# Windowed attention with sinks and a gated MLP on one core: the order of all five queues, the engines of movable work and the PSUM banks written out as tables in place of a list scheduler

## The chip, the cores and the metric

The kernel runs on one core of one Trainium2 chip. Its time is the device time of one execution in microseconds (us); less is better. A core has five engines, each with an instruction queue of its own that is worked through in order: TensorE (PE, matmuls; its weight loads are shown as PEld), VectorE (DVE), ScalarE (ACT), GpSimd (POOL) and SyncE (SP, which here only issues DMAs). They tell each other of finished work through semaphores. PSUM, where matmuls leave their results, has 8 banks of 128 partitions x 2 KB; in this kernel POOL reads none of them.

## The reference, cut to what matters

Attention over 4 batches x 8 heads x 768 positions with head size 64, in which a query sees the first 4 positions (sinks) and the 128 newest; then a gated MLP over the 3072 tokens with d_model 512 and d_ff 2048.

```python
B, H, S, D = q.shape                                   # 4, 8, 768, 64
scores = (1.0 / np.sqrt(D)) * np.matmul(q, k.transpose(0, 1, 3, 2))
rel = pos[:, None] - pos[None, :]
keep = (pos[None, :] < 4) | ((rel >= 0) & (rel < 128))
a = softmax(np.where(keep, scores, -1e9))              # over the last axis
x = np.matmul(a, v).transpose(0, 2, 1, 3).reshape(3072, 512)
h = x @ w_in                                           # 512 -> 2048
g = h * (1.0 / (1.0 + np.exp(-beta * h)))
out = g @ w_out                                        # 2048 -> 512
```

## The kernel before

**The work.** The tokens are cut into 8 half batches (hb, and T_ in the MLP) of 384 tokens. Attention goes by units: unit u is a pair of heads in half batch u // 4, so hb 0 has units 0 to 3, and so on to 31. The groups of matmuls on PE have these names here:

- T (lines 773 to 800, units 0 to 11): six transposes on PE that make q and k of a unit head-size-major, and their copy out of PSUM. From hb 3 on a DMA transpose does this (XP, line 764, called X).
- S (SC, 869 to 971): a burst of score matmuls for one to three tiles (L930, and L885 for the narrow bands from unit 8 on). Each tile takes two PSUM banks; ACT takes the exponential of both (E, L947), and DVE or POOL multiplies or selects the mask (L956, L966 on DVE, L962 on POOL; from unit 8 on most masks can be done on POOL alone). SS (L978, L982) is the same for the sink keys of a half batch.
- A (AV, 1005 to 1044): attention times v for one unit, or for four units as a quad (L1007, L1023, L1034), then a reciprocal and a multiplication on DVE (L1038, L1040).
- R (OT, 1046 to 1065): the result transposed into xT, on PE with a copy by DVE or ACT for units 0 to 11, later by a DMA transpose that SP issues (L1054).
- H (HQ, 1070 to 1088): four matmuls of 384 columns (L1078) for one block m of 16 of one tile T_; ACT's tanh (L1084) and DVE's product g (L1086) follow. H2.15 is T_ 2, m 15. There are three buffers for t and three for g.
- O (OQ, 1093 to 1121): g times w_out for tile 0 and the last third of tile 7, four matmuls at a time (L1102). O0.1.2 is tile 0, third 1, quarter 2.
- W (WP, 1228 to 1279): all other thirds go in pairs, a pair by seven products of half the size (L1245, eight matmuls of 256 columns each) instead of eight. W3.6 is product 6 of pair 3. The products need sums and differences of g (s_op, L1167) on DVE or POOL and of w_out (w_sums, L1150), and additions behind them (L1253). Pairs 0, 1, 3, 4, 6, 7, 9 are inside tiles 1 to 7; pairs 2, 5 and 8 join the last thirds of tiles 1 and 2, 3 and 4, 5 and 6.

**Loads and casts.** SP issues the loads of q, k and v (line 656), of the weights in 16 pieces (load_w, L668) and the DMA transposes; ACT issues the four loads of k of hb 0. The casts to bf16 (cast, cast_w, lines 571 to 577) run on ACT, DVE or POOL.

**What sets the order.** _program (431) calls these functions in an order that is partly written out ("early", "later", lines 1509 to 1525) and partly decided by background() (1387), which lets loads, casts and sums in when a running estimate says so. take() and choose() (528 to 562) give PSUM banks by the same estimate. Each call records operations with an estimated duration and, for movable work, a choice of engines (any_of, 500). Then Graph.arrange() (176 to 292) builds all queues anew: a list scheduler that keeps an estimated clock for each engine and for DMA, may take one of the next 3 to 10 groups of PE, picks for movable work the engine that would be done first, keeps POOL and some DVE operations (lock) apart, and puts in fill matmuls (L1494) in the first 18 us. resolve() (294) turns dependences into semaphore waits; a wait for work on the same engine is dropped for PE, and for the others unless it reads what was written.

The order that came of it on PE, from T5 on:

```
T5 T4 T7 H0.0 H0.1 T6 H0.2 H0.3 S[5,6] SS H0.4-0.6 S[7,8] H0.9 H0.7 H0.8 H0.10 S[9,10] H0.11-0.14 A5 A4 A6 A7 H0.15
O0.0.0 O0.1.0 R4 O0.2.0 O0.0.1 R5 R6 O0.1.1 R7 O0.2.1 H1.0-1.9 O0.0.2 T8 T9 O0.1.2 O0.2.2 T10 S[11,12] O0.0.3 T11
O0.1.3 O0.2.3 S[13,14] S[15] SS H1.10-1.12 A8 A9 H1.13 R8 H1.14 A10 A11 H1.15 R9 W0.1 R10 W0.2 W0.6 R11 W0.7 H2.0
S[16,17,18] SS W0.5 W0.4 W0.3 H2.1 S[19,20,21] H2.2-2.8 A12-15 H2.9-2.15 W1.1 S[22,23,24] W1.6 W1.2 W1.7 S[25,26] SS
W1.5 W1.4 A16 A17 H3.0 H3.1 W1.3 A18 A19 W2.1 H3.2 H3.3 W2.6 W2.2 H3.4-3.6 W2.7 H3.7 W2.5 H3.8 H3.9 W2.4 H3.10-3.12
W2.3 H3.13-3.15 W3.1 S[27,28,29] SS W3.2 W3.6 W3.5 W3.7 S[30,31,32] W3.4 H4.1 H4.2 H4.0 H4.3-4.7 W3.3 H4.8-4.15 A20-23
W4.1 W4.6 W4.2 S[33,34,35] W4.7 W4.5 W4.4 S[36,37] SS W4.3 W5.1 H5.0 H5.1 A24 H5.2 W5.6 H5.3 A25 A26 A27 W5.2 W5.7
H5.4 W5.5 H5.5-5.14 W5.4 H5.15 W5.3 W6.1 S[38,39,40] SS W6.2 W6.6 H6.0 S[41,42,43] W6.7 H6.1-6.7 A28-31 W6.5 W6.4
H6.8-6.15 W6.3 H7.0 W7.1 H7.1 H7.2 W7.6 W7.2 W7.7 W7.5 H7.3-7.5 W7.4 W7.3 H7.6 W8.1 H7.7 H7.8 W8.6 H7.9 W8.2 H7.10
H7.11 W8.7 H7.12-7.15 W8.5 W8.4 W9.1 W8.3 W9.6 W9.2 W9.7 W9.5 W9.4 W9.3, then the last third of tile 7 (O7.2, twice four)
```

Of the kernel before, what the change touches and what calls it, by code (L numbers as in the profile page):

```python
# [22 lines left out]
class Op:  # L23
    __slots__ = ("eng", "fn", "deps", "signal", "count", "waits", "sem", "vc", "dma", "seq", "end", "ns", "alts",
                 "group", "tail", "hold", "lock", "chain", "preds", "ready", "left", "succ", "at")


class Graph:

    ENGINES = ("pe", "act", "dve", "gp", "sp")
    HOP = 180
    SKIP = 3
    PAD = 100
    STRICT = 1
    WIDE, EARLY = 10, 60000
    SLACK = 0  # L40
    YIELD = 500
    COLD, WARM = 217, 150

    def __init__(self):
        self.ops = []
        self.writers = {}
        self.readers = {}
        self.last_x = {}
        self.free = {e: 800.0 for e in self.ENGINES}
        self.dma_free = 2500.0  # L50
        self.stalls = [(16000.0, 1100.0), (34000.0, 700.0)]
        self.port = {"gp": 0.0, "dve": 0.0}
        self.gaps = {"act": [], "dve": [], "gp": []}
        self.group = 0
        self.filler, self.fill_to = None, 0

    def begin(self):

        self.group += 1

    def add(self, eng, fn, ns=0, r=(), w=(), x=(), dma=None, alts=None, after=(), hold=550, chain=None, lock=False):

        o = Op()
        if alts:
            fn, ns = alts[eng]
        o.eng, o.fn, o.dma, o.ns, o.alts = eng, fn, dma, ns, alts or {eng: (fn, ns)}
        o.signal, o.count, o.waits, o.vc, o.hold, o.chain = False, 0, [], None, hold, chain
        o.group = self.group if eng == "pe" else None  # L70
        o.lock = lock
        o.seq = len(self.ops)
        deps = []
        for k in r:
            ws = self.writers.get(k)
            assert ws, k
            deps += [(p, True) for p in ws]
        for k in w:
            deps += [(p, False) for p in self.readers.get(k, ())]
            deps += [(p, False) for p in self.writers.get(k, ())]  # L80
        for k in after:
            deps += [(p, False) for p in self.readers.get(k, []) + self.writers.get(k, [])]
        for k in x:
            deps += [(p, False) for p in self.last_x.get(k, ())]
        o.deps = deps
# [5 lines left out]
        for k in x:  # L91
            self.last_x[k] = [o] if eng == "pe" else self.last_x[k] + [o]
        o.at = 0.0
        self.place_early(o, eng)
        self.ops.append(o)
        return o

    def ready_at(self, o, eng):
        return max([0.0] + [p.end + (0 if p.eng == eng and not p.dma else self.HOP) for p, _ in o.deps])

    def slot(self, eng, t, ns):

        for i, (a, b) in enumerate(self.gaps[eng]):
            if max(a, t) + ns <= b:
                return max(a, t), i
        return max(self.free[eng], t), None

    def place_early(self, o, eng):

        if eng in ("pe", "sp") or o.dma:  # L110
            self.place(o, max(self.free[eng], self.ready_at(o, eng)))
            return
        if o.alts and len(o.alts) > 1:
            best = None
            for e, (fn, ns) in o.alts.items():
                at, i = self.slot(e, self.ready_at(o, e), ns)
                if best is None or at + ns < best[0]:
                    best = (at + ns, e, at, i)
            _, eng, at, i = best
            o.eng = eng  # L120
            o.fn, o.ns = o.alts[eng]
        else:
            at, i = self.slot(eng, self.ready_at(o, eng), o.ns)
        gaps = self.gaps[eng]
        if i is None:
            if at > self.free[eng] + 50:
                gaps.append((self.free[eng], at))
                del gaps[:-40]
            self.free[eng] = at + o.ns
        else:  # L130
            a, b = gaps.pop(i)
            gaps[i:i] = [g for g in ((a, at), (at + o.ns, b)) if g[1] - g[0] > 50]
        o.at, o.end = at, at + o.ns

    def fill(self, fn, r):

        def one():
            o = Op()
            wide = self.free["pe"] + 2 * self.filler[0] <= self.fill_by
            o.eng, o.fn, o.dma, o.ns = "pe", fn[wide], None, self.filler[0] * (1 + wide)  # L140
            o.signal, o.count, o.waits, o.vc, o.lock = False, 0, [], None, False
            o.deps = [(p, True) for k in r for p in self.writers[k]]
            return o
# [19 lines left out]
    def at(self, keys):  # L163

        t = 0.0
        for k in keys:
            ws = self.writers.get(k)
            if not ws:
                return None
# [1405 lines left out]
```

## Time and profile before

| what | value |
|---|---|
| three runs | 222.39 us median, 221.91 to 224.91 |
| the profiled execution's own time | 221.55 us |
| its span in the profile | 219.8 us |
| granted TensorE clock | 1.00 |
| DMA moved | 39.92 MB, mean 182 GB/s |

The span runs from the first to the last instruction that the profile shows. Its page gives busy time by engine, then groups of instructions by line; further views give busy time by stretch, the chain of waits that ended last (a piece is start, length, what), and the timeline, where brackets say how long the engine was idle before a piece and what ended that. A matmul's busy time includes its way through the array, so matmuls in a row overlap and busy times add up to less than the sum of their lengths. DVE, ACT and POOL instructions in a row overlap a little, too.

### The profile page before, as it was taken

The numbers are of one execution on the slowest core, as the hardware profiler recorded it, in microseconds if no ns is written. First come the engines' busy times: TensorE is split into PE (matmuls) and PEld (weight loads), VectorE is DVE, ScalarE is ACT, GpSimd is POOL, SyncE is SP. The second block draws the span as 40 slices with busy tenths as digits, with TensorE's granted clock in tenths as the row PEclk, the third lists the DMA queues.
The fourth block names the chain that finished last, engine by engine and source line by source line (L and its number), as shares of the span: only waits on it lengthen the run. The fifth ranks groups of instructions, "written<-read, shape, count | busy, mean of one in ns | idle before, by whom it ended". The sixth has DMA issues, their size and how long they took to land.

```text
span 219.8 us, 5396 instructions
## 1 busy us (share of the span) xinstructions
PE 209.0 (95%) x2155; PEld 141.5 (64%) x2155; DVE 173.8 (79%) x375; ACT 152.8 (70%) x261; POOL 82.7 (38%) x136
## 2 busy tenths in 40 slices
PE   8899999998988999899998999999999999999995
PEld 3456547554456756578765766778676576777883
DVE  2686999899697549999868598999885698957850
ACT  3698996896993998767567797585959837355401
POOL 7225560382651693080011691582006930010010
DMA  6999999999969999899649999669947233120023
GB/s 186 251 329 369 352 277 372 364 282 220 194 156 179 217 148 260 139 184 215 144 123 228 221 109 220 125 134 244 145 102 171 44 86 84 48 94 6 0 99 143
DMA packets 94721, 39.92 MB, mean 182 GB/s; under 512 B 82072, under 2 KB 89512, under 8 KB 94696
## 3 DMA queue, kind: packets, MB, share of 16 engines
q1 hardware_dynamic: 91928, 33.28, 70.4%
q0 software_dynamic: 1680, 5.51, 7.4%
q10 hardware_dynamic: 1088, 0.79, 1.1%
q8 instruction: 17, 0.28, 0.6%
q14 instruction: 8, 0.07, 0.1%
HBM read 27.37 MB, written 6.29 MB: 153 GB/s over the span
## 4 chain that ended last, share of the span: by engine, by line
PE 54%; DVE 20%; DMA 10%; SPq 7%; ACT 6%; issue 2%
PE P L1245 22%; PE P L1078 22%; DVE g L1086 9%; SPq L656 5%; DMA g<-in_moe_w_in_dram 4%; DMA g<-in_moe_w_out_dram 4%; PE P L1102 4%; PE P L1034 3%; ACT t L1084 3%; ACT E L947 2%; DMA v_stage<-in_v_dram 2%; PE P L885 2%; DVE g L1167 1%; DVE onorm L1040 1%; SPq L668 1%
## 5 line engine op out<-in xcount | busy, mean ns | idle before, releaser
L1078 PE MATMUL P<-xT,w_in 128*128 128x384 bf16 x512 | 91.3, 326 | 2.0 <-DVE g L1086 0.8
L1084 ACT ACTIVATE t<-P,hbeta 128x384 f32<-128x384 f32 x128 | 70.9, 590 | 28.3 <-PE P L1078 19.3
L1086 DVE SCALAR_TENSOR_TENSOR g<-t,P 128x384 bf16<-128x384 f32 x128 | 67.2, 548 | 20.0 <-ACT t L1084 16.8
L1078 PEld LDWEIGHTS P<-xT,w_in 128*128 128x128 bf16 x512 | 48.4, 98 | 33.9 <-DVE g L1086 3.4
L962 POOL TENSOR_SCALAR_AFFINE_SELECT E<-E 128x512 bf16<-128x512 bf16 x57 | 39.2, 715 | 28.8 <-ACT E L947 28.6
L947 ACT ACTIVATE E<-P 128x1024 bf16<-128x1024 f32 x44 | 43.3, 1033 | 3.7 <-PE P L885 3.4
L1245 PE MATMUL P<-w_out,g 128*128 128x256 bf16 x240 | 30.7, 273 | 1.4 <-DVE g L1086 1.1
L1276 POOL DMA_DIRECT2D out_dram<-osb x18 | 9.9, 549 | 58.6 <-DVE osb L1253 58.5
L1245 PEld LDWEIGHTS P<-w_out,g 128*128 128x128 bf16 x240 | 22.7, 98 | 6.1 <-DVE g L1086 1.8
L1040 DVE TENSOR_TENSOR onorm<-P,rden 128x384 bf16<-128x384 f32 x32 | 17.6, 555 | 0.7
L1102 PE MATMUL P<-w_out,g 128*128 128x512 bf16 (+2 forms) x80 | 15.3, 337 | 0.0
L1253 DVE TENSOR_TENSOR osb<-P,wst 128x256 f32<-128x256 f32 x30 | 12.2, 417 | 3.7 <-PE P L1245 3.5
L1034 PE MATMUL P<-vaug,E 128*128 128x65 bf16 x352 | 14.4, 193 | 0.0
L1034 PEld LDWEIGHTS P<-vaug,E 128*128 128x128 bf16 x352 | 13.6, 97 | 1.1
L1494 PE MATMUL P<-const-bfloat16-1.0 128*128 128x512 bf16 (+1 forms) x37 | 10.9, 417 | 0.8 <-PEq L1557 0.8
L1245 PE MATMUL P<-v_stage,g 128*128 128x256 bf16 x80 | 10.4, 273 | 0.4 <-DVE wst L1253 0.4
L1253 DVE TENSOR_TENSOR wst<-P,wst 128x256 f32<-128x256 f32 x20 | 8.3, 417 | 2.8 <-PE P L1245 2.8
L1245 PE MATMUL P<-wst,g 128*128 128x256 bf16 x80 | 10.4, 273 | 0.0
L1102 PEld LDWEIGHTS P<-w_out,g 128*128 128x128 bf16 x80 | 6.9, 98 | 5.2
L571 ACT ACTIVATE k<-k_stage 128x512 bf16<-128x512 f32 (+1 forms) x12 | 7.4, 616 | 3.7 <-DMA k_stage<-in_k_dram 3.7
L956 DVE TENSOR_TENSOR E<-E,maskS 128x512 bf16<-128x512 bf16 x16 | 7.6, 487 | 2.0 <-ACT E L947 2.0
L571 ACT ACTIVATE wst<-P 128x256 f32<-128x256 f32 x9 | 3.4, 383 | 8.1 <-PE P L1245 8.0
(99 smaller groups left out, 259.4 us busy)
## 6 DMA issues: line engine op xcount, KB each, us to landing
v_stage<-in_v_dram SPq DMA_DIRECT2D x24, 256.0 KB, 5.3
out_dram<-osb POOLq DMA_DIRECT2D x21, 256.0 KB, 3.4
q_stage<-in_q_dram SPq DMA_DIRECT2D x15, 256.0 KB, 5.2
k_stage<-in_k_dram SPq DMA_DIRECT2D x15, 256.0 KB, 5.2
wst<-in_moe_w_in_dram SPq DMA_DIRECT2D x5, 512.0 KB, 8.1
wst<-in_moe_w_out_dram SPq DMA_DIRECT2D x4, 512.0 KB, 7.9
g<-in_moe_w_out_dram SPq DMA_DIRECT2D x4, 512.0 KB, 6.6
q_stage<-in_q_dram SPq DMA_DIRECT2D x2, 768.0 KB, 7.7
```

Source lines behind the costliest of these rows:

```text
L656: add("act" if hb == 0 and n == "k" and Q2 else "sp", lambda e: e.dma_start(dst, src), ns, w=keys, dma=f"d{n}{z}{'' if i is None else i}", ...
L947: add("act", lambda e, src=src, dst_=dst_: e.activation(dst_, src, AF.Exp, bias=0.0, scale=SCALE), act_ns(1024), w=[("E", z)] + [("m", z, ...
L962: alts = {"gp": (lambda e, dd=dd, sg=sg: e.affine_select(dd, dd, [[0, n] for n in dd.shape[1:-1]] + [[sg, 128]], ALU.is_ge, 0.0, base=min( ...
L1034: e.matmul(A[:, c0:c0 + D + 1], E[t_ % NE][:, i, hh, :], vaug[vz][:, kb % NK, 2 * hp + hh, :], start=a, stop=o, skip_group_check=True), 31,
L1040: add("dve", lambda e: e.tensor_tensor(onorm[on][:, :, :, :].rearrange("p m h d -> p (m h) d"), av[:, :, 0:D], rden[on][:, :].unsqueeze(2) ...
L1078: add("pe", lambda e, c=c: e.matmul(hp, w_in16[:, c, m * 128:(m + 1) * 128], xT[:, c, t0:t0 + HALF], start=(c == 0), stop=(c == 3)), mm_ns ...
L1084: add("act", lambda e: e.activation(tt[ti][:, :], hp, AF.Tanh, bias=0.0, scale=hbeta[:, m:m + 1]), act_ns(HALF) + 93, r=["hbeta"], w=[("t" ...
L1086: add("dve", lambda e: e.scalar_tensor_tensor(gt[T_ % NG][:, m, :], tt[ti][:, :], 1.0, hp, ALU.add, ALU.mult), dve_ns(HALF), r=[("t", ti)] ...
L1102: add("pe", lambda e, m=m: e.matmul(P[:, bk, 0:n], gt[T_ % NG][:, m, t * 128:(t + 1) * 128], w_out16[:, m, cols], start=(m == 0), stop=(m ...
L1245: add("pe", lambda e, i=i: e.matmul(P[:, bk, 0:HN], lhs[:, i, :], rhs[:, i, :], start=p in (1, 6, 5, 4) and i == 0, stop=i == 7, skip_grou ...
L1253: add("dve", lambda e: e.tensor_tensor(d, src, u, ALU.add), 310, r=r, w=w, x=[("B", bk)], after=after)
L1494: G.fill([lambda e, n=n: e.matmul(P[:, 7, 0:128 * n], one.to_broadcast([128, 128]), one.to_broadcast([128, 128 * n]), start=True, stop=Tru ...
```

## The change

The list scheduler, the estimates, the choice of banks and background() are gone. In their place stand four tables: SCRIPT, one letter a call, says in which order the functions record their operations; PE_ORDER says the order of the groups on PE, one letter a group, with the fill matmuls (f, F) in it; BANKS gives the PSUM bank of each take; QUEUES lists for ACT, DVE, POOL (gp) and SP the recorded operations in order, two base-36 digits each, and thereby their engine. What the functions compute, and their tiles, are as before. In resolve() a wait for work on the same engine is now dropped for PE alone.

```diff
-    G = Graph()
-    _program(nc, G, sb, ps, q, k, v, moe_w_in, moe_w_out, moe_beta, out)
-    G.arrange()
+    G = Graph(BANKS)
+    fillers = _program(nc, G, sb, ps, q, k, v, moe_w_in, moe_w_out, moe_beta, out)
+    G.order(PE_ORDER, QUEUES, fillers)
     G.resolve()
...
+class Bank(int):
+    def __new__(cls, bank):
+        b = super().__new__(cls, bank)
+        b.last, b.used = [], False
+        return b
...
+    def take(self, n):
+        return [Bank(next(self.banks)) for _ in range(n)]
...
+    def order(self, pe, queues, fillers):
+        last, at = {}, {}
+        lists = {e: [] for e in self.ENGINES}
+        for c in pe:
+            if c in fillers:
+                lists["pe"].append(self.new("pe", fillers[c]))
+                continue
+            i = at[c] = at.get(c, -1) + 1
+            while not self.by_kind[c][i]:
+                i = at[c] = i + 1
+            for o, takes in self.by_kind[c][i]:
+                for t in takes:
+                    if not t.used and t in last:
+                        o.deps += [(p, False) for p in last[t].last]
+                    t.used = True
+                    last[int(t)] = t
+                lists["pe"].append(o)
+        for e, s in queues.items():
+            for i in range(0, len(s), 2):
+                o = self.loose[int(s[i:i + 2], 36)]
+                o.eng, o.fn = e, o.alts[e]
+                lists[e].append(o)
...
     def resolve(self):
...
-                if not p.dma and p.eng == o.eng and (p.eng == "pe" or not raw):
+                if not p.dma and p.eng == o.eng == "pe":
                     continue
...
+PE_ORDER = ("FFFFFFFFFFF.FFF.FFF..FFFF..Ff....FF.FFFf...FFf..f.FF.Ff.BTTTTHHSHHSHHHHSHHHHHHHHAAARAOORRROHHHHOHHHO"
...
+QUEUES = {"act": ("010z03050718131b151e171k1l1n1q1w1z1t3334352a372d2e2f2k3g3u3n3d3h3y413l3j3x4f3p4c3v44464p4m484a3a4k4i"
...
-    for c in later:
...
+    for c in SCRIPT:
+        do(c)
+    return fillers
```

Read out with the groups' names, PE's order from T4 on is now:

```
T4 T5 T6 T7 H0.0 H0.1 S[5,6] SS H0.2 H0.3 S[7,8] H0.4-0.7 S[9,10] H0.8-0.15 A4 A5 A6 R4 A7 O0.0.0 O0.1.0 R5 R6 R7 O0.2.0
H1.0-1.3 O0.0.1 H1.4-1.6 O0.1.1 O0.2.1 H1.7 O0.0.2 O0.1.2 O0.2.2 T8 T9 T10 O0.0.3 O0.1.3 H1.8 T11 H1.9-1.15 O0.2.3
S[11,12] W0.1 S[13,14] W0.6 W0.2 W0.7 S[15] SS W0.5 W0.4 A8 A9 W0.3 A10 R8 A11 R9 R10 S[16,17,18] SS R11 H2.0-2.15
S[19,20,21] W1.1 W1.6 W1.2 W1.7 W1.5 W1.4 A12-15 W1.3 W2.1 W2.6 W2.2 S[22,23,24] W2.7 W2.5 W2.4 S[25,26] SS W2.3 A16 A17
H3.0-3.4 A18 H3.5 A19 H3.6-3.15 H4.0-4.8 W3.1 S[27,28,29] SS W3.6 W3.2 W3.7 S[30,31,32] W3.5 H4.9-4.14 W3.4 H4.15 W3.3
W4.1 A20-23 W4.6 W4.2 W4.7 S[33,34,35] W4.5 W4.4 W4.3 S[36,37] SS W5.1 W5.6 W5.2 H5.0-5.7 W5.7 H5.8-5.10 A24 H5.11-5.14
W5.5 A25 H5.15 A26 A27 W5.4 W5.3 W6.1 S[38,39,40] SS W6.6 W6.2 W6.7 S[41,42,43] W6.5 H6.0-6.15 W6.4 A28-31 W6.3 W7.1 W7.6
W7.2 W7.7 W7.5 W7.4 W7.3 W8.1 W8.6 H7.0-7.15 W8.2 W8.7 W8.5 W8.4 W8.3 W9.1 W9.6 W9.2 W9.7 W9.5 W9.4 W9.3, then O7.2
```

Instructions by kind of work and engine, where they differ (DMA issues are on the same engines as before):

| work | ACT | DVE | POOL |
|---|---|---|---|
| casts of q, k, v | 33 to 26 | 32 to 23 | 9 to 25 |
| casts of weights | 5 to 6 | 6 to 6 | 6 to 5 |
| masks | - | 31 to 24 | 57 to 64 |
| sums of g (L1167) | - | 38 to 34 | 2 to 6 |
| sums of w_out (L1150) | - | 5 to 6 | 3 to 2 |
| copies to xT (R) | 11 to 8 | 1 to 4 | - |
| copies and additions of O and W | 20 to 19 | 55 to 56 | - |

On the queues that matter beside PE: ACT casts weight pieces 8 and 9 behind H0.12, 10 behind H0.15, 13 behind H1.3 and 15 behind H1.4; before, 9 behind H0.14, 12 behind R4, 13 behind R6 and 14 behind R7. POOL has, behind its first weight sum, two q casts of hb 2 and then its second weight sum, where it had a weight sum, one q cast and a weight sum; and it does all six casts of q and k of hb 3 before the masks of S[11,12] to S[15]. SP issues the third v load of hb 2 and the sink values of batch 2 behind the first DMA transpose of hb 3, and mixes v loads and transposes differently later; its order up to the last weight load is unchanged. In a run of H groups ACT's and DVE's tables follow the groups, with neighbours exchanged here and there (H2.1 before H2.0).

More of the change, by code (lines that the diff above doesn't have):

```diff
@@ L23 @@
 class Op:
[L24 to L25 removed]
+    __slots__ = ("eng", "fn", "deps", "signal", "count", "waits", "sem", "vc", "dma", "seq", "alts", "done")
+class Bank(int):
[3 more added lines that the diff above has]
+        return b
 class Graph:
     ENGINES = ("pe", "act", "dve", "gp", "sp")
[L35 removed]
@@ L36, with __init__ @@
[L36 to L55, printed above, removed]
+    def __init__(self, banks):
+        self.banks = iter(banks)
+        self.ops, self.loose, self.groups = [], [], []
+        self.writers, self.readers = {}, {}
+        self.kind, self.by_kind = ".", {}
@@ L108, in place_early @@
[L108 to L143, printed above, removed]
-        self.filler, self.fill_to = (self.COLD, one), self.group
-    def shut(self, o, eng):
-        return self.port["gp" if eng == "dve" else "dve"] if eng == "gp" or eng == "dve" and o.lock else 0.0
@@ L1203, in sums_when @@
                 return
[L1204 to L1205 removed]
+            do("s")
     pairs_done = [0]
```

554 lines of the change are left out of this document (134 added, 420 removed).

## The prediction

> **What bounds the kernel now.** I read the page first, then busy time by stretch, then the chain of waits, and last the timeline at the places where TensorE breaks off.
>
> ```profile
> span 219.8 us, 5396 instructions
> PE 209.0 (95%) x2155; PEld 141.5 (64%) x2155; DVE 173.8 (79%) x375; ACT 152.8 (70%) x261; POOL 82.7 (38%) x136
> ```
>
> ```profile
> 18.50:36.50 18.00, 17.32 (x195) 10.88 (x194) 16.06 (x36) 17.06 (x29) 8.16 (x9) 1.00 1.05 337
> 36.50:51.50 15.00, 14.12 (x89) 7.77 (x87) 13.99 (x29) 11.45 (x19) 7.59 (x4) 1.00 1.08 316
> 51.50:71.60 20.10, 18.55 (x211) 11.60 (x211) 16.57 (x37) 14.86 (x26) 7.68 (x13) 1.00 1.04 186
> 71.60:91.60 20.00, 18.55 (x253) 11.97 (x252) 14.33 (x33) 17.02 (x29) 10.61 (x18) 1.00 1.11 201
> 91.60:96.90 5.30, 5.26 (x60) 4.22 (x61) 5.30 (x10) 4.88 (x7) 3.03 (x4) 1.00 0.83 133
> 96.90:122.70 25.80, 24.90 (x250) 17.98 (x248) 21.15 (x46) 16.26 (x29) 5.83 (x10) 1.00 0.93 184
> 122.70:140.20 17.50, 17.50 (x197) 12.05 (x196) 14.70 (x33) 12.68 (x22) 10.76 (x15) 1.00 1.04 177
> 140.20:168.60 28.40, 28.06 (x313) 20.47 (x312) 24.80 (x52) 21.94 (x37) 9.38 (x14) 1.00 0.67 145
> 168.60:213.70 45.10, 44.89 (x418) 33.85 (x418) 34.78 (x73) 22.96 (x41) 11.28 (x17) 1.00 0.23 66
> ```
>
> The columns are stretch, length, then busy time of PE, PEld, DVE, ACT, POOL, the granted clock (1.00 throughout), DMA share and GB/s. TensorE (PE) is the bound, and DVE, ACT and DMA in the first two rows are nearly as full. PE's idle time looks small, but a broken run hides more. The next rows are pieces of the chain of waits and, below, four of PE's timeline.
>
> ```profile
> 51.96 1.73 PE P L1102 x8
> 53.68 0.34 PE P L781 x6
> 82.06 0.34 PE P L1007 x9
> 82.40 1.56 PE P L1034 x48
> 122.77 0.62 PE P L885 x24
> 130.45 5.20 PE P L1078 x32
> 140.28 0.97 PE P L885 x24
> 144.00 0.51 PE P L885 x16
> 205.11 8.73 PE P L1245 x80
> 213.84 3.51 PE P L1102 x32
> ```
>
> ```profile
> 50.72 0.90 PE L781 MATMUL P<-ident,k 128*128 128x128 bf16 x3 [0.67 <-DVE k L576]
> 60.25 0.82 PE L1078 MATMUL P<-xT,w_in 128*128 128x384 bf16 x4 [0.23 <-ACT E L947]
> 89.73 1.05 PE L1245 MATMUL P<-w_out,g 128*128 128x256 bf16 x8 [0.80 <-DVE g L1086]
> 168.34 0.34 PE L1078 MATMUL P<-xT,w_in 128*128 128x384 bf16 x1 [0.32 <-DMA xT<-onorm]
> ```
>
> Unbroken, four matmuls of L1078 (an H group) take 5.20 / 8 = 0.65; alone the same four show 0.82. So every break costs its idle time plus about 0.16 that the busy column hides. Without a break PE needs, from T4/T5 at 18.5 to the last tile: 128 H groups x 0.65 = 83.2; 70 product groups (W, L1245) x 0.873 = 61.1; 12 groups O x 0.865 = 10.4; T 8 x 0.34 and R 8 x 0.17 = 4.1; A groups about 12.5 (a quad is 0.34 + 1.56); S bursts about 10.4 (0.51 to 0.97 each). Together 181.7; the last tile's 3.51 stays apart. PE reached that tile at 213.84, so it lost 213.84 - 18.5 - 181.7 = 13.6 us. This is all that an order can win; before 18.5, and after 213.84, both orders are alike.
>
> **The change part by part.** Nothing of the scheduler runs on the chip; matmul, fill and DMA counts are unchanged, and the five queues agree until R3, at 18.5 us: nothing there. The new rule in resolve() keeps waits of an engine for itself; built, DVE has 61 of these against 59, POOL 8 against 8, and a producer long retired costs nothing (bounds 0 and two instruction tails, 0.2): 0. Explicit banks cost nothing by themselves; where a bank comes back late I count it below.
>
> Engines. DVE loses 15 operations (7 masks, 9 casts, 4 sums less; 5 copies and additions more), ACT 10 (casts, xT copies), POOL gains 25: 7 masks, 16 casts, 4 sums, less a weight cast and a weight sum.
>
> ```profile
> L962 POOL TENSOR_SCALAR_AFFINE_SELECT E<-E 128x512 bf16<-128x512 bf16 x57 | 39.2, 715 | 28.8 <-ACT E L947 28.6
> L573 POOL TENSOR_SCALAR_AFFINE_SELECT vaug<-v_stage 128x512 bf16<-128x512 f32 x3 | 2.0, 656 | 7.5 <-DMA v_stage<-in_v_dram 7.5
> L1150 POOL TENSOR_TENSOR q_stage<-w_out 128x1024 bf16<-128x1024 bf16 x2 | 4.3, 2130 | 9.8 <-DVE w_out L577 9.8
> L1086 DVE SCALAR_TENSOR_TENSOR g<-t,P 128x384 bf16<-128x384 f32 x128 | 67.2, 548 | 20.0 <-ACT t L1084 16.8
> L571 ACT ACTIVATE xT<-P 128x384 bf16<-128x384 bf16 x11 | 5.4, 493 | 2.6 <-PE P L1060 2.6
> ```
>
> On POOL this is 7 x 0.715 + 16 x 0.656 + 4 x 2.13 - 1.05 - 2.13 = +20.8 us. POOL is idle 137 us of the span and waits 28.6 us for the exponentials alone, so the work itself is covered; if that cover went, A groups would wait, since every A needs its last mask. What DVE and ACT save, some 9 and 5 us, is worth only what PE waits less, so it is no term of its own.
>
> The rates that decide the waits:
>
> ```profile
> 161.45 0.59 ACT t L1084
> 162.06 0.55 DVE g L1086
> 90.17 0.70 DVE v_stage L1167
> 90.89 0.70 DVE wst L1167
> ```
>
> ```profile
> 35.04 1.06 ACT L571 ACTIVATE w_out<-g 128x1024 bf16<-128x1024 f32 x1
> 76.69 2.85 ACT L947 ACTIVATE E<-P 128x1024 bf16<-128x1024 f32 x3 [0.27 <-PE P L885]
> 79.41 3.42 ACT L1084 ACTIVATE t<-P,hbeta 128x384 f32<-128x384 f32 x7
> 49.25 2.08 DVE L576 CAST k<-k_stage 128x512 bf16<-128x512 f32 x3
> 47.00 1.11 POOL L573 TENSOR_SCALAR_AFFINE_SELECT q<-q_stage 128x512 bf16<-128x512 f32 x1
> 48.09 2.29 POOL L1150 TENSOR_TENSOR k_stage<-w_out,q_stage 128x1024 bf16<-128x1024 bf16 x1
> ```
>
> In a row ACT does a tanh every (3.42 - 0.59) / 6 = 0.47 and an exponential every 0.91 (the first ends after 1.03); a sum follows a sum after 0.6. One H costs PE 0.65, so long runs of H (now up to 25, before at most 10) leave ACT 0.18 a group to catch up. The stretches above are cut where PE starts O0.0.0, T9, S[16,17,18], W1.6, A16, S[30,31,32], S[33,34,35], S[41,42,43] and the last tile. The length of a stretch less its groups at the unbroken rates is what it lost: 2.0, 1.4, 3.2, 2.6, 0.2, 1.8, 0.4, 1.2 and 0.8, the 13.6 again. I walk the new queues from place to place in the same way and note by how much PE is behind an unbroken order so far.
>
> - O0.0.0 (first use of w_out): before 2.0 behind, at 36.5. Now A4 to A7 and all H0 are done earlier, but this group needs the weight cast j=9, which ACT can only do when it lands: 35.04 + 1.06 = 36.1. PE starts at 36.2 instead of 34.7: 1.5. The wait moves from H and S to this load. SP's queue is the same up to here.
> - T9: before 3.4 behind, because the k cast at 49.25 (1.41 of the 2.08) was slow and T8 waited 0.67 idle. POOL's weight sum at 48.09 lay beside it. Now POOL has two q casts and then its weight sum at about 47.8 again, and DVE two k casts, ACT one. If they collide as before T9 starts at 51.2, if not at 50.3. I take 50.8, as the two lie equally near: 2.3.
> - S[16,17,18]: before 6.6 behind: eight breaks, at H1.12, R8, H1.14, W0.1, W0.2, W0.6, W0.7 and W0.5. Now pair 0 is done ahead of A8, between the bursts. The last H1 to W0.6 needs 0.59 + 0.55 + 0.6 + 0.7 and hops, 2.6, and O, S, W0.1 and S (2.8) cover it. Late are S[13,14] (a bank of an exponential, 0.4), R10 (0.2) and S[16,17,18] itself (R9's copy of 0.49 on ACT: 0.3). A8 and A10 get their last masks from POOL, which first has six casts of q and k; the casts end about 59, the masks are ready just in time. With the breaks' rest 3.4.
> - W1.6: before 9.2 behind (89.73 shows 0.80 of it). Now H2.0 waits 0.75 for the first exponential's bank; ACT then needs 3 x 0.91 + 0.37 + 16 x 0.47 + 2 casts x 0.52 = 11.6 for what PE does in 10.7, so S[19,20,21] waits 0.65 for H2.14's bank, and W1.6 0.3 for the two sums behind H2.15. 5.3.
> - A16: 9.4 before; now 6.1: W2.4 waits 0.35 for banks of three exponentials, A16 0.1, the bursts' turns 0.3.
> - S[30,31,32]: 11.2 before. The 25 H of tiles 3 and 4 run unbroken; then S[27,28,29] waits 0.45 for H4.8's bank and W3.6 0.95 for the first exponential: 7.6.
> - S[33,34,35]: 11.6 and 7.9, S[41,42,43]: 12.8 and 9.6 (W4.4 0.3, W6.6 0.9, again first exponentials).
> - The last tile: 13.6 and 9.6. Before, H6.0 waited for xT (168.34); now SP, by the walk, is through hb 7's transposes some 4 us sooner, and the H7 run has pair 8's remaining products behind it.
>
> SP: L2v2 and a small load go behind the first of hb 3's transposes, so v for A8 is issued later, at about 57, with A8 at 66: covered. The weights' order is unchanged. So 13.6 - 9.6 = 4.0 us go, and 221.55 (the profiled execution) gives 217.6. The three runs shown have their median 0.84 above that execution, 222.39; the lowest is 0.36 above. I leave the 217.6 and let the range hold the rest.
>
> By the Trainium skill (GPSIMD Engine Reference, 8. Key points), POOL shares its SBUF interfaces with VectorE and contends with DVE operations of two SBUF inputs or in a two-port mode; the k cast above agrees, and g, which reads PSUM, keeps 548 ns. The same page (4.1 Engine selection) puts two-input work at about twice DVE's time on GpSimd; the trace has 2130 ns against 700, three times, and that decides. By its factor of two the four sums would be 2.9 us cheaper on POOL, which is covered either way.
>
> **The rivals.**
> First, the moved work is paid back by DVE. POOL beside DVE costs up to about 1.0 (1.41 where 0.42 is usual), and 25 more POOL operations meet DVE's remaining casts, masks and sums. Most of the moved sums stand beside operations that read PSUM, against it; the T8 collision and the s1 chain speak for it. If four collisions of 0.6 fall on waits PE feels, 4.0 shrinks to 1.6: 220.0. This is what the skill's sentence on the shared interfaces would make of it.
> Second, the walk counts too many waits: bank and exponential waits of 0.3 to 0.95 rest on mean latencies, and the first exponential after a burst may start earlier if ACT is ahead. If the collision at T8 and half of the later waits go, another 3 us: 214.6.
> Third, slower: POOL becomes the engine that PE waits for. Its queue is in order, and the masks for A8 stand behind the k cast of a load that is issued only when hb 2's casts are done. If that load lands 3 us late, A8 to R11, and with them H2, slip; the same again at C4 before A12 and X7 before S[38,39,40]. It decides once two or three such places lose over 4.0 together; three of 3 us less 4.0 is 5 us more: 226.6. DMA share of 1.04 to 1.11 until 91.6 speaks for it, margins of 1 to 2 us at each against.
> The change does what it says: the orders do differ on every engine after R3; nothing could make it void.
>
> **How the numbers follow.** Forecast as walked 0.50, its own range 216.3 to 219.2; paid back 0.18; fewer waits 0.26; slower 0.06. Within 2%, 217.94 to 226.84, is about what a measurement of this kernel can tell from no change. Of the forecast somewhat over half lies below 217.94: 0.30, with the second rival's 0.26 and a little of the first 0.57; slower by over 2%: half of the third and what I have not seen, 0.05; the rest 0.38. The range goes from the second rival's 214.6 to a little beyond the first, 220.4.
>
> **What would show it.** Right: PE's last tile (L1102) at about 209.8; L1078 in runs of 64 and more; O0.0.0 released by the ACT cast of w_out; T8 by a k cast; H2.0, W3.6 and W6.6 by an exponential; POOL about 103 us busy, DVE below 166 and ACT below 149. Wrong: A groups released by POOL, POOL waiting for DMA of k_stage before masks, S bursts waiting for DMA transposes, or DVE casts and sums near 1 us as a rule.

## The result, and the profile after

The changed kernel takes 221.61 us (median of 20 runs), the kernel before 222.66 us (20 runs). The ratio is 0.9941, with a 95% interval of 0.9913 to 0.9968: some 1.3 us less, where 4.0 were forecast, and the time lies outside the range that was given (214.6 to 220.4). The medians are 1.05 us apart, because the ratio leaves out three slower executions, two of the changed kernel and one of the other. The profiled execution of the changed kernel took 222.21 us. Its page begins:

```profile
span 220.5 us, 5410 instructions
PE 208.2 (94%) x2150; PEld 142.1 (64%) x2155; DVE 169.7 (77%) x360; ACT 147.7 (67%) x251; POOL 102.2 (46%) x161
```

POOL's 102.2 us are the forecast 103, ACT's are below 149 as forecast, DVE's are not below 166. Next, busy time by stretch, with the prediction's columns and cut where TensorE starts the same groups: B (the transpose of beta just ahead of T4, up to which the queues agree), O0.0.0, T9, S[16,17,18], W1.6, A16, S[30,31,32], S[33,34,35], S[41,42,43] and the last tile. (What lies inside a stretch differs between the kernels.)

```profile
19.20:38.40 19.20, 17.36 (x198) 11.06 (x199) 15.84 (x33) 17.43 (x30) 9.69 (x12) 1.00 1.01 325
38.40:53.20 14.80, 13.89 (x82) 7.43 (x83) 14.11 (x28) 9.90 (x17) 5.94 (x4) 1.00 1.05 303
53.20:72.60 19.40, 19.11 (x224) 13.30 (x224) 16.24 (x35) 15.34 (x26) 9.42 (x17) 1.00 0.87 162
72.60:87.50 14.90, 13.73 (x145) 8.39 (x145) 11.20 (x24) 14.33 (x26) 9.18 (x16) 1.00 1.18 222
87.50:102.30 14.80, 14.80 (x216) 12.46 (x216) 11.04 (x27) 7.37 (x13) 9.15 (x13) 1.00 0.75 143
102.30:126.50 24.20, 23.13 (x218) 14.77 (x216) 18.76 (x40) 19.88 (x34) 13.79 (x17) 1.00 1.01 166
126.50:141.40 14.90, 13.62 (x177) 10.11 (x176) 11.43 (x29) 8.24 (x14) 7.49 (x13) 1.00 1.13 181
141.40:169.40 28.00, 27.12 (x312) 20.05 (x312) 23.20 (x49) 19.20 (x31) 14.91 (x17) 1.00 0.84 162
169.40:214.30 44.90, 44.77 (x413) 33.15 (x413) 35.44 (x72) 22.33 (x41) 14.18 (x21) 1.00 0.27 81
```

The last tile starts at 214.33, not at 209.8. The stretch from 87.50 has no idle time on TensorE at all; the two stretches from 102.30 to 141.40 have 2.35 us of it, and the first two 2.75. What TensorE waited for, by the waits view (engine, line, releaser: us in total, times, longest; of the lines of 0.5 us and more, three that lie wholly or in part ahead of B are left out):

```profile
PE P L879 <- DVE w_in L403: 1.3, 1, 1.3
PE P L696 <- DMA qkT<-q: 0.9, 1, 0.9
PE P L1042 <- DVE wst L965: 0.8, 1, 0.8
PE P L606 <- DVE k L403: 0.8, 1, 0.8
PE P L879 <- DMA xT<-onorm: 0.6, 1, 0.6
PE P L1042 <- ACT E L753: 0.5, 1, 0.5
```

In order: H0.12 waits for a cast of a w_in piece, S[33,34,35] for a transpose of hb 6, W1.6 for its sums, T8 for a k cast, H4.0 for a transpose into xT (its third and fourth matmuls; the recorded expectations below call this place H4.1), W6.6 for an exponential. The first, second and fifth are nowhere in the forecast, and a burst that waits for a DMA transpose was among its signs of being wrong. W4.6 waits 0.4 for its sums, which the forecast does not have either. No line names POOL, so the third rival (masks late on POOL) did not come.

Each kernel was profiled twice more, because executions differ. The table gives what TensorE lost against an unbroken order, in us: the distance between the starts of two groups, less the groups between them at the prediction's rates.

| stretch | before, three profiles | forecast | after, three profiles |
|---|---|---|---|
| B to O0.0.0 | 2.16, 2.00, 2.29 | 1.5 | 3.19, 2.97, 2.91 |
| O0.0.0 to T9 | 1.38, 2.37, 1.82 | 0.8 | 0.97, 1.60, 1.17 |
| T9 to A16 | 6.00, 6.02, 6.00 | 3.8 | 3.14, 3.40, 3.44 |
| A16 to S[33,34,35] | 2.17, 2.16, 2.16 | 1.8 | 4.08, 5.60, 3.81 |
| S[33,34,35] to the last tile | 1.99, 3.90, 2.15 | 1.7 | 2.30, 1.48, 1.50 |
| sum | 13.70, 16.45, 14.42 | 9.6 | 13.68, 15.05, 12.83 |

So the mean sum fell from 14.9 to 13.9, which agrees with the times. 2.7 us were won from T9 to A16, more than forecast, and 2.3 given back from A16 to S[33,34,35]; the start to T9 won nothing.

### The profile page after: what moved, and what is told of

It reads as the page before. It is cut to its first block, busy times and chain, and to the rows that moved or that the text cites. A ratio compares the mean times of both kernels' runs of the same rounds, so it can differ in the third digit from the quotient of the medians.

```text
span 220.5 us, 5410 instructions
## 1 busy us (share of the span) xinstructions
PE 208.2 (94%) x2150; PEld 142.1 (64%) x2155; DVE 169.7 (77%) x360; ACT 147.7 (67%) x251; POOL 102.2 (46%) x161
## 4 chain that ended last, share of the span: by engine, by line
PE 31%; DMA 11%; DVE 5%; ACT 2%; POOL 2%; SPq 1%; issue 1%
PE P L1042 14%; PE P L879 13%; DVE g L887 3%; DMA v_stage<-in_v_dram 3%; DMA out_dram<-osb 3%; DMA qkT<-q 2%; DMA xT<-onorm 2%; PE P L902 2%; DMA q_stage<-in_q_dram 2%; PE P L837 2%; ACT t L885 1%; POOL E L768 1%; POOL wst L965 1%; DVE g L965 1%; PE P L696 1%; SPq L482 1%
## 5 line engine op out<-in xcount | busy, mean ns | idle before, releaser
L879 PE MATMUL P<-xT,w_in 128*128 128x384 bf16 x512 | 88.1, 326 | 2.5 <-DVE w_in L403 1.3
L885 ACT ACTIVATE t<-P,hbeta 128x384 f32<-128x384 f32 x128 | 69.8, 587 | 20.3 <-PE P L879 12.7
L887 DVE SCALAR_TENSOR_TENSOR g<-t,P 128x384 bf16<-128x384 f32 x128 | 65.2, 548 | 18.3 <-ACT t L885 17.0
L768 POOL TENSOR_SCALAR_AFFINE_SELECT E<-E 128x512 bf16<-128x512 bf16 x61 | 40.3, 689 | 25.8 <-ACT E L753 25.7
L837 PE MATMUL P<-vaug,E 128*128 128x65 bf16 x352 | 15.2, 193 | 0.2 <-DVE vaug L403 0.2
L902 PE MATMUL P<-w_out,g 128*128 128x512 bf16 (+2 forms) x77 | 14.5, 335 | 0.2
L400 POOL TENSOR_SCALAR_AFFINE_SELECT q<-q_stage 128x512 bf16<-128x512 f32 x9 | 6.3, 709 | 11.4 <-DMA q_stage<-in_q_dram 11.4
L965 POOL TENSOR_TENSOR g<-g 128x1024 bf16<-128x1024 bf16 x3 | 7.4, 2458 | 8.0 <-DVE v_stage L965 6.4
L398 ACT ACTIVATE wst<-P 128x256 f32<-128x256 f32 x6 | 2.3, 387 | 12.2 <-PE P L1042 12.2
L696 PE MATMUL P<-qkT 64*64 64x192 bf16 (+3 forms) x336 | 8.9, 234 | 1.5 <-DMA qkT<-q 0.9
```

What stands on the lines that cost most here:

```text
L768: alts = {"gp": (lambda e, dd=dd, sg=sg: e.affine_select(dd, dd, [[0, n] for n in dd.shape[1:-1]] + [[sg, 128]], ALU.is_ge, 0.0, base=min( ...
L837: e.matmul(A[:, c0:c0 + D + 1], E[t_ % NE][:, i, hh, :], vaug[vz][:, kb % NK, 2 * hp + hh, :], start=a, stop=o, skip_group_check=True), 31,
L879: add("pe", lambda e, c=c: e.matmul(hp, w_in16[:, c, m * 128:(m + 1) * 128], xT[:, c, t0:t0 + HALF], start=(c == 0), stop=(c == 3)), mm_ns ...
L885: add("act", lambda e: e.activation(tt[ti][:, :], hp, AF.Tanh, bias=0.0, scale=hbeta[:, m:m + 1]), act_ns(HALF) + 93, r=["hbeta"], w=[("t" ...
L887: add("dve", lambda e: e.scalar_tensor_tensor(gt[T_ % NG][:, m, :], tt[ti][:, :], 1.0, hp, ALU.add, ALU.mult), dve_ns(HALF), r=[("t", ti)] ...
L902: add("pe", lambda e, m=m: e.matmul(P[:, bk, 0:n], gt[T_ % NG][:, m, t * 128:(t + 1) * 128], w_out16[:, m, cols], start=(m == 0), stop=(m ...
```

## The experiments

Ratios are to the kernel before, run beside each on the same chip, with 95% intervals; the changed kernel stands at 0.9941 (0.9913 to 0.9968). Diffs of tables are written with names: L6q0 is the load of the first third of q for hb 6, C its cast, X its DMA transpose, R16 the transpose of unit 16 into xT, s4.2 the second sum of pair 4.

**The executions themselves.** e1, e2, e14 and e15 are the two kernels unchanged.

> The kernel before, unchanged, profiled once more. Theory A (the profiled execution that the forecast stood on was a lucky one: its third q load landed at 7.09 us, in the execution of the changed kernel at 7.77, and every later load followed): this execution lies near the median 222.7, its early loads land 0.3 to 0.8 us later, and TensorE's last tile starts near 214.8 instead of 213.7. Theory B (the two executions differ by their kernels alone): landings as in the first profile to 0.2 us, and the last tile within 0.3 of 213.7.

> The changed kernel, unchanged, profiled once more. Theory A (luck of the first loads): loads land earlier than in its first profile, H0.12 waits less than the 1.3 us it waited for its weight piece, and the last tile starts near 213.5. Theory C (the order itself makes late transposes): the waits for DMA transposes before H4.1 (0.6 us) and before S[33,34,35] (0.9 us), and the wait for a k cast at T8 (0.75), are there again, whatever the first loads do.

> The changed kernel, unchanged, a third profile. Both theories: 220 to 224 us. If the loss between A16 and S[33,34,35] belongs to the order, it is 3 us or more once more (4.1 and 5.6 before); by chance, anything from 1.5 up.

> The kernel before, unchanged, a third profile. 221.5 to 224.5 us; from S[27,28,29] to S[33,34,35] it lost 1.3 us in both profiles so far and does so again, if its order takes late loads better than the tables; ACT waits 2 us or less for loads of v.

They took 224.18 and 222.68 (before), 224.02 and 220.54 (after). The queues of both kernels are the same up to B, yet B starts at 18.50, 18.36 and 18.90 in the one and at 19.18, 19.52 and 18.34 in the other, and the k load that T8 needs lands at 49.07, 49.78 and 50.26, and at 50.38, 51.32 and 49.45. Landings thus differ by 1 to 2 us between executions, and theory A is right in so far as the forecast stood on the best of three executions of the kernel before. Its course of events did not come: in e1 the third q load landed at 6.71, sooner than the 7.09 of the first profile, and the last tile still started at 216.3, against 213.7; in e2 it landed at 8.10, later than 7.77. Late landings don't explain the shortfall either, since they hit both kernels. e2 and e14 show H4.0's wait again:

```profile
116.96 0.34 PE L879 MATMUL P<-xT,w_in 128*128 128x384 bf16 x1 [1.12 <-DMA xT<-onorm]
```

```profile
115.12 2.12 PE L879 MATMUL P<-xT,w_in 128*128 128x384 bf16 x12 [0.57 <-DMA xT<-onorm]
```

The wait of S[33,34,35] for a transpose came in e2 (0.85 idle) and hardly in e14 (0.12), where W4.1 waited 0.6 instead. From A16 to S[33,34,35] the kernel before loses 2.16 or 2.17 in all three, the changed one 3.81 and more. That loss goes with the order, though its size does not: kernels of the tests below whose queues are the changed one's from hb 3 on lost 1.86 (e11), 3.43 (e16) and 4.96 (e6) there.

**e3, e7, e12: the engine moves undone, all or in part.**

```diff
- act, dve, gp queues of the changed kernel
+ e3: each movable operation whose engine changed back on its engine of before
+ e7: only 8 masks and 6 sums, POOL to DVE (a mask and two sums that had gone the other way stay on DVE)
+ e12: only C3q0-2, C3k0-1, C4k0, C4q1, C3v2, C7v1: POOL to DVE; C3k2, C4k2, C5q2, C5k0-1, C6q0, C7k1: POOL to ACT
```

> The changed kernel with every movable operation on the engine that it had before, put into that engine's queue at the time at which it ran; the order on TensorE, the banks and SyncE's queue stay. Theory D (the first rival: POOL's added work is paid back by DVE operations that it slows): faster than the changed kernel by 0.6 to 1.6 us, 220.0 to 221.0, with the DVE sums and casts that took 1 to 2.3 us back near 0.4 to 0.7. Theory C (what was lost sits in SyncE's order and the DMA transposes): within 0.5 us of 221.6, with the waits at H4.1 and S[33,34,35] still there. If the moves are what bought the gain: slower, 222.5 or more.

> The changed kernel with only the masks and the sums of g that went from DVE to POOL back on DVE, at the time at which they ran; casts, weight sums and all orders stay. Theory D (POOL's added masks and sums are paid back by DVE): faster by 0.5 to 1.5 us, ratio 0.987 to 0.992. Theory as forecast (they are covered on POOL and would press on DVE): the same to 1 us slower, ratio 0.994 to 0.998. If it is like the test of all engines, much slower, the place is a DVE operation with products g behind it.

> The changed kernel with only the 16 casts of hb 3 to 7 that went to POOL back on DVE (9) and ACT (7), put where they ran. Theory E (the casts are the part of the engine moves that counts, because a cast that waits for its load holds up products g or tanh behind it on DVE or ACT, and nothing urgent on POOL): slower than the changed kernel by 2 us or more, ratio above 1.003, with DVE and ACT waiting for DMA of q_stage or k_stage. Rival (the 14 us of the test of all engines came from the weight casts, the copies and the additions): ratio within 0.004 of 0.994.

Measured: e3 1.0591 (1.0536 to 1.0647), e7 0.9956 (0.9923 to 0.9989), e12 1.0031 (0.9999 to 1.0063). Masks and sums make no difference that shows, so the first rival falls as a general price. The 16 casts on POOL are worth some 0.9%, 2 us. In e3 ACT stands longest before a v cast that waits for its load:

```profile
ACT vaug L401 <- DMA v_stage<-in_v_dram: 8.4, 2, 5.8
```

One such wait is 5.8 us long, with tanh behind it. In e12 DVE's and ACT's waits for k loads are 1.7 and 2.4 us, against 0.9 and 0.4 in the changed kernel; DVE's wait for q loads is 5.8, against 5.9. Theory E's size is confirmed there, its mechanism for k loads alone. Why the rest of e3's 14 us went was not followed further: an order that suits one choice of engines may not suit another.

**e6, e16: the collision at T8 undone.**

```diff
  gp:  ... C2q1 C2q2
-      w_sum3
  dve: ... w_sum5 ...
-      w_sum6 C2k0 C2k1 w_sum8
+      C2k0 C2k1 w_sum6 w_sum8 w_sum3
```

> The changed kernel with the collision at T8 undone: the third weight sum goes from POOL to DVE, and DVE does its last three weight sums behind the two k casts that T8 waits for. Theory D (the shared port made this step cost its full price): the weight sum that took 2.3 us on DVE takes 0.7, the k casts start when the load lands, T8's wait of 0.75 to 1.2 us shrinks under 0.3, and T9 starts about 1.0 us sooner against the first loads; if that lasts to the end the ratio is 0.989 to 0.991. Rival (DMA bounds TensorE up to about 53 us and the loads behind it set the pace again): T9 comes sooner, S[11,12] to S[16,17,18] take the time back, ratio 0.993 to 0.996.

> The run in which only T8's collision is undone, once more. If the collision is worth what the local times say (T9 1.2 us sooner against the loads), the ratio is 0.985 to 0.990; if its first result was helped by few runs, 0.990 to 0.994.

Measured: 0.9873 (0.9815 to 0.9930) and 0.9899 (0.9845 to 0.9953). The timeline of the changed kernel at T8, of POOL, DVE and TensorE:

```profile
49.66 2.12 POOL L948 TENSOR_TENSOR v_stage<-w_out 128x1024 bf16<-128x1024 bf16 x1
```

```profile
50.02 2.31 DVE L948 TENSOR_TENSOR k_stage<-w_out,q_stage 128x1024 bf16<-128x1024 bf16 x1
52.26 0.75 DVE L403 CAST k<-k_stage 128x512 bf16<-128x512 f32 x2
```

```profile
52.73 0.62 PE L606 MATMUL P<-ident,k 128*128 128x128 bf16 x3 [0.75 <-DVE k L403]
```

and of e16, DVE and TensorE:

```profile
50.49 0.76 DVE L407 CAST k<-k_stage 128x512 bf16<-128x512 f32 x2 [0.29 <-DMA k_stage<-in_k_dram]
51.16 0.68 DVE L952 TENSOR_TENSOR k_stage<-w_out,q_stage 128x1024 bf16<-128x1024 bf16 x1
```

```profile
51.51 0.33 PE L610 MATMUL P<-ident,k 128*128 128x128 bf16 x3
```

Beside POOL's sum, DVE's takes 2.31 us and the k casts stand behind it; alone it takes 0.68. By the Trainium skill (GPSIMD Engine Reference, 8. Key points) the two engines contend in this way where a DVE operation has two SBUF inputs; the trace agrees, 2.31 against 0.68. The edit takes away POOL's sum and also puts DVE's behind the casts, so it does not separate the two: a sum of 0.68 from 50.02 on would have held the casts by some 0.3 us beyond the landing at 50.38 (an estimate from these rows). T9 is 2.03 and 2.53 late (behind an unbroken order from B) in e6 and e16, against 4.08 to 4.57; part of that was won ahead of O0.0.0, where the edit changes nothing. From O0.0.0 to T9 alone, the seven kernels with this repair lost -0.16 to 0.38, the three profiles of the changed one 0.97 to 1.60: about 1.2 us. Some 0.5 of it is lost again by A16 (3.8 on average from T9, against 3.3). The last tile is 12.36 and 12.46 late in e6 and e16. The seven kernels with this repair have a mean ratio of 0.9901, and six without (the changed one, e4, e5, e7, e9, e11; e3 and e12, which move casts back, are left out) 0.9947: 1.0 us.

**e11: a load moved.**

```diff
  sp: ... LW6
- L1v2 LW7
+ LW7 L1v2
```

> The changed kernel with the load of the weight piece that H0.12 waits for one place sooner in SyncE's queue, ahead of a v load. If TensorE is bound by all loads up to about 53 us: the piece lands 1.0 to 1.3 us sooner, H0.12 waits less by that, but A4 to O0.0.0 wait more (their v pieces and the first w_out pieces land as before), O0.0.0 starts as far behind its w_out piece's landing as in the other runs (1.5 to 3.5 us) and the ratio stays within 0.003 of 0.994. If the one load was the bound: O0.0.0 and all behind it 0.8 to 1.2 us sooner, ratio 0.988 to 0.990.

0.9952 (0.9924 to 0.9979). H0.12 no longer waits, but neither does it in e6, e8 and e12, which leave that load where it was; A4 waits 0.45 us for a v cast, and O0.0.0 is 1.95 late, as in e12 (1.91) and e13 (1.82), which do not have the edit. No gain shows, as expected where all loads set the pace up to there; the run does not prove that they do.

**e4, e5, e8, e9, e10, e13: the waits between A16 and S[33,34,35].**

```diff
  sp:  (e4, e8, e9, e10, e13)
- L5k2 X5q0 R17 R16 L6q0 R18 R19 X5k2 ...
+ L5k2 R16 R17 R18 R19 X5q0 L6q0 X5k2 ...
  sp:  (e8, e9, e10, e13; e4 has all three L5v last)
- L6q2 L6k2 L5v0 L6k1 L6k0 L5v1 L6q1 L5v2
+ L6q2 L6k2 L5v0 L6k1 L6k0 L6q1 L5v1 L5v2
  gp:  (e5, e8: each store of pairs 0 to 6 where its rows are ready; e9, e10, e13: the last store of pair 1
       behind s3.3, those of pair 2 behind masks of S[27] to S[30])
  dve: (e8, e9, e10, e13)
- s4.1 s4.3 s4.2
+ s4.1 s4.2 s4.3
  dve: (e8, e9, e10: C6k2 C5v0 C6k0; e9, e10, e13: C7q2 behind W4.5; e13: C5v0, C6k0 behind H4.11, H4.12)
  act: (e13)
- H4.9 H4.11 C5v1 H4.10 H4.12 H4.14 H4.13 H4.15 C6q1 C5v2
+ H4.9 H4.11 H4.10 H4.12 C6q1 H4.14 C5v1 H4.13 H4.15 C5v2
  sp:  (e13) X6 in the order q0 q2 k2 k1 q1 k0
  e8, e10, e13: with T8's repair
```

> The changed kernel with two stretches of SyncE's queue put in another order: the four transposes of units 16 to 19 into xT ahead of the first transpose of hb 5 and of a load of hb 6, and the q and k loads of hb 6 ahead of the three v loads of hb 5. Theory C: the waits before H4.1 and S[33,34,35] shrink by 1.0 to 1.8 us together and the time falls by as much, to 219.8 to 220.6. Rival (TensorE would wait at the next place anyway, because ACT or DVE is just behind): the waits move to W4.6, S[38,39,40] or W6.6 and the time stays within 0.4 us of 221.6.

> The changed kernel with one difference: the output stores of pairs 0 to 6 stand in POOL's queue where their rows are finished, and not 8 to 32 us later (the last store of pair 1 was ready at 93.9 us and issued at 126.2). Theory S (the late stores hold the output buffers that W3.2 to W3.5 write, so that DVE stands before a store with products g behind it, and lie beside the transposes that S[33,34,35] needs): DVE's waits for a store (1.3 and 2.3 us in the two profiles) vanish, the last transpose for S[33,34,35] lands 2 to 3 us sooner, its 0.9 us of waiting goes, and the time falls by 0.8 to 2.0 us, to a ratio of 0.985 to 0.990 to the kernel before. Rival (the stores collide with other transposes wherever they stand): waits move to H4.1 or S[27,28,29] and the ratio stays at 0.994.

> The changed kernel with four repairs together: the stores of pairs 0 to 6 at once, the transposes of units 16 to 19 ahead of hb 5's first transpose (and four q and k loads of hb 6 ahead of two v loads of hb 5, with two casts exchanged on DVE), the second sum of pair 4 ahead of its third, and the weight sums at T8 as in the test of that alone. If the waits of H4.1 (1.0 to 1.6 us), W4.6 (0.6), S[33,34,35] (1.0), DVE's store wait (0 to 1.0) and T8 (1.0) are each on the path that sets the end, they add to 3 to 4 us: ratio 0.975 to 0.982, about the 217.6 that was forecast. If each is absorbed at the next place, ratio 0.990 or more.

> The changed kernel with its queues between 100 and 150 us put in another order, T8's collision left in: the transposes of units 16 to 19 ahead of hb 5's first transpose; four loads of hb 6 ahead of two v loads; on DVE the v cast of hb 5 between two k casts, the second sum of pair 4 ahead of the third and a q cast of hb 7 behind an addition of W4.5; on POOL the stores of pairs 1 and 2 some 5 to 13 us sooner, between masks. Theory C (late transposes, stores and casts that wait for loads in front of g): from A16 to S[33,34,35] TensorE loses 2 us or less instead of 4.1 and 5.6, and the ratio is 0.980 to 0.988. Rival (waits move on, as in the test of early stores): 3.5 us or more there, ratio 0.990 to 0.996.

> The same with T8's collision undone as well. If the two add up: ratio 0.975 to 0.982, T9 about 2.0 us behind an unbroken order and the last tile 10 to 11 behind, near the 9.6 that was forecast. If they do not add up (the loads bound TensorE again): 0.985 or more.

> The kernel with both repairs (queues between 100 and 150 us, T8's weight sums), and in addition the casts of hb 5's v and hb 6's k and q, which waited 2 to 3 us for their loads in front of H4.9 to H4.15 on DVE and ACT, stand 1 to 4 groups further behind there; the transposes of hb 6 follow in the order in which their casts come. Theory F (casts that wait for loads in front of tanh and g): the wait of W4.1 (1.0 to 1.5 us in three runs) shrinks under 0.5, TensorE loses 2.0 us or less from A16 to S[33,34,35], ratio 0.980 to 0.987. Rival (chance of the execution): 3.0 to 3.5 lost there as in the two runs without this, ratio 0.988 to 0.993.

Measured: e4 0.9904 (0.9865 to 0.9942), e5 0.9982 (0.9951 to 1.0014), e8 0.9923 (0.9891 to 0.9955), e9 0.9945 (0.9914 to 0.9975), e10 0.9913 (0.9882 to 0.9944), e13 0.9856 (0.9804 to 0.9908). From A16 to S[33,34,35] e4 lost 4.01, e8 2.96, e10 3.47 and e13 3.36. In each of these, and in e18, H4.0's wait is gone; with SyncE's queue left alone there it came in six of ten profiles. Each time a wait at another place had taken over. e4's ratio is what theory C asked for, but its interval meets the changed kernel's, and in its trace W3.4 waits 1.7 us. e8 and e10 came out as the branch in which the repairs do not add up, e9's ratio as its rival. In e10 it is W4.1 that waits, because a v cast stands before tanh on ACT (ACT, then TensorE):

```profile
130.53 0.63 ACT L402 ACTIVATE vaug<-v_stage 128x512 bf16<-128x512 f32 x1 [2.38 <-DMA v_stage<-in_v_dram]
131.06 2.45 ACT L889 ACTIVATE t<-P,hbeta 128x384 f32<-128x384 f32 x5
```

```profile
133.22 1.05 PE L1046 MATMUL P<-w_out,g 128*128 128x256 bf16 x8 [1.33 <-DVE g L891]
```

In e13 that wait is gone too, as theory F said, and S[33,34,35] waits for the transpose that its edit made last:

```profile
139.18 0.80 PE L700 MATMUL P<-qkT 64*64 64x256 bf16 x32 [1.55 <-DMA qkT<-k]
```

Theory S was half right. In the changed kernel the stores stand in POOL's queue 0.3 to 32 us behind their rows, and DVE does stand before one of them, with a product g behind it (here e14):

```profile
131.94 0.42 DVE L1050 TENSOR_TENSOR osb<-P,wst 128x256 f32<-128x256 f32 x1 [1.94 <-DMA out_dram<-osb]
132.28 1.01 DVE L887 SCALAR_TENSOR_TENSOR g<-t,P 128x384 bf16<-128x384 f32 x2
```

With the stores at once (e5) DVE's wait for a store is gone, but H4.0 and S[33,34,35] wait as before, W4.3 waits 1.2 us more, and the ratio is no better: the rival.

**e17, e18: loads off SyncE's queue.**

```diff
- sp: L5v0 L5v1 L5v2 L6v0 L6v1 L6v2
+ gp: the same six at the times at which they were issued (e17: on e6's kernel; e18: on e13's)
```

> The changed kernel with T8's collision undone (0.987 and 0.990 by itself) and the six v loads of hb 5 and 6 issued by POOL at the times at which SyncE issued them; all else as it was. Theory G (SyncE, which issues without a gap there, is the bound): the last transpose for S[33,34,35] is issued 2.5 to 3.5 us sooner against TensorE, that wait goes, TensorE loses 2.5 us or less from A16 to S[33,34,35] (4.96 and 3.43 without), ratio 0.980 to 0.985. Rival (DMA itself or the casts are the bound): transposes are issued sooner but land as late, or the wait moves to W4.1 or A20; 3.4 us or more, ratio 0.987 to 0.991.

> The kernel of the test with casts behind (0.9856 by itself, 3.36 us lost from A16 to S[33,34,35], 1.7 of it waiting for the last transpose) with the same six v loads on POOL. Theory G: the 1.7 us before S[33,34,35] go for the most part, 2.0 us or less are lost there, ratio 0.977 to 0.983. Rival: as in the run before, 0.984 to 0.988.

0.9930 (0.9896 to 0.9964) and 0.9911 (0.9870 to 0.9952). In e18 the wait before S[33,34,35] shrinks from 1.7 to 0.15 us and W3.5 loses 1.1 instead (2.55 lost from A16); in e17 S[33,34,35] still waits 1.6 us (4.52 lost). The waits view names a DVE sum there, but that ended 0.25 us ahead of the burst; the last transpose, issued 4.9 us ahead of it (3.3 and 2.7 in e6 and e16), took 6.5 us to land, 0.09 ahead. It was issued sooner and landed as late, as the rival has it. Theory G falls as the one cause.

## Why the forecast was wrong, step by step

**T9 to A16: right.** The walk gave 3.8 lost, 3.1 to 3.4 were. Pair 0 stands ahead of A8, H runs without breaks, and most of what was won stands in this stretch; no run takes that part of the order back by itself. That the sum came so close is in part luck: waits on first exponentials (W3.6, W6.6, H2.0) are there, at 0.1 to 0.7 instead of 0.75 to 0.95, and W1.6 loses 0.93 where 0.3 was taken. The last stretch, 1.5 to 2.3 against 1.7, is right as well.

**O0.0.0: wrong by 1.4 to 1.7 us.** The step took the w_out cast as the last arrival. But the new order does H0.8 to H0.15 in a row, and TensorE comes to H0.12 before its weight piece has been cast. The timelines of DVE and TensorE after:

```profile
31.63 1.07 DVE L403 CAST w_in<-wst 128x1024 bf16<-128x1024 f32 x1 [0.73 <-DMA wst<-in_moe_w_in_dram]
```

```profile
32.76 0.99 PE L879 MATMUL P<-xT,w_in 128*128 128x384 bf16 x5 [1.30 <-DVE w_in L403]
```

In the trace of before that piece landed at 30.53; by the prediction's rates an unbroken H0.12 would have come at 29.6. The number was there, and the step asked one load only. This wait (1.30 in two profiles after, 0.33 in the third) is about what the step had put at O0.0.0 itself; the rest stands where it put nothing: turns of bursts, and A4 with a v cast (0.2 to 0.6 idle). How much is lost here goes with the execution: the experiments whose queues are the changed kernel's up to here lost 1.82 to 2.96.

**T9: the choice between two ends.** The prediction took the middle of "collides" and "does not". It collides in all three profiles (T8 to T9 loses 1.2 to 1.6), though not as before: it is DVE's weight sum that is slow, with the k casts behind it. About 1.2 us come back up to T9 where that is undone, 1.0 in the ratios. This is what of the first rival came true, at one place.

**S[30,31,32] and S[33,34,35]: wrong by 2.0 to 3.8 us, the largest part.** The step said of SyncE that it was covered, and looked at its queue up to hb 3 alone. SyncE's issues (the profile does not count them as busy) of the kernel before, then of the changed one, with the bursts that need them:

```profile
106.06 2.58 SPq L764 DMA_TRANSPOSE qkT<-k  x2
133.10 1.38 SPq L764 DMA_TRANSPOSE qkT<-q  x1
```

```profile
117.51 0.70 PE L885 MATMUL P<-qkT 64*64 64x192 bf16 x32
140.22 0.98 PE L885 MATMUL P<-qkT 64*64 64x256 bf16 x31
```

```profile
118.38 1.26 SPq L589 DMA_TRANSPOSE qkT<-k  x1
135.84 1.29 SPq L589 DMA_TRANSPOSE qkT<-q  x1
```

```profile
122.27 0.52 PE L696 MATMUL P<-qkT 64*64 64x192 bf16 x16
141.44 0.76 PE L696 MATMUL P<-qkT 64*64 64x256 bf16 x31 [0.89 <-DMA qkT<-q]
```

Before, the last transpose of hb 5 is issued 8.9 us ahead of S[27,28,29] and that of hb 6 5.7 ahead of S[33,34,35]; after, 2.6 and 4.3. In their landings the lead is plainer: the last transpose for S[33,34,35] had landed 3.5 us ahead of the burst in all three profiles of before. In all three after, and in 14 of the 17 profiles of the changed kernel and its variants, the burst starts 0.09 to 0.11 us behind that landing, so it is this transpose that lets it start. A12 to A15 come 10 us later on TensorE (91.9 instead of 81.8), their transposes into xT stand ahead of loads of hb 5 in SyncE's queue, and everything behind it (transposes, loads of hb 6, their casts, their transposes) lost its lead. With no lead left, whatever is next in a queue shows: a transpose at H4.0, a store or a cast at W4.1, a transpose at S[33,34,35]. That each wait can be removed and that others take over is shown by e4, e8, e10, e13 and e18 (2.55 to 4.01 lost, not clearly less than 1.86 to 5.60 without them); that the lost lead is the common cause is argued from these rows and the three even profiles of before, and not shown by a run that restores it throughout. e18 comes nearest: there the transposes land 2.3 us ahead of S[33,34,35], and W3.5 waits for a DVE addition instead. Which of DMA, SyncE and the casts would bound a better order stays open.

**The base.** 221.55 us, the execution that the sum was made against, was 1.1 under the median of 20 runs. A forecast of the same gain from 222.66 would have read 218.7.

**Better versions.** e13 (0.9856) lies below the changed kernel with intervals that do not meet; e6 and e16 (0.9873, 0.9899), with one edit, overlap with e13, and e18, built on e13, gave 0.9911. That T8's repair helps is clear from the two groups of kernels and the stretch from O0.0.0 to T9; how much the rest adds is not.

## What to carry to other kernels

An order that lets TensorE run unbroken has to be checked against the lead of every stream that feeds it, the queue that only issues DMAs included: for each group the slack between landing and use, and not only whether it lands in time. In queues worked in order, a cast that waits for its load belongs on an engine with nothing urgent behind it, or behind the work that does not need it. Where a forecast has two ends and the profile already shows the worse one at that very place, take the worse one, and take several executions before trusting a base to 1 us.

## What was not expected of the hardware

In the changed kernel's trace a DMA transpose of 128 x 512 holds SyncE for 1.26 us, about twice a 256 KB load (0.58 at the shortest), and SyncE has no gap over 0.9 us from 104 to 138 us. Beside two output stores, the last two transposes of hb 6 landed 5.5 and 6.5 us after their issue; the median was 2.5 us between 113 and 122 us. In six profiles of the two kernels, whose queues agree up to there, the third piece of k of hb 0 landed between 7.30 and 9.18 us.
